# Attention scores of the last four head pairs from float32r parts, in row halves of the array

## The chip, the cores and the metric

The kernel runs on one core of a Trainium2 chip. The metric is the device time of one execution in microseconds. Before the change the median of three runs is 1076.69 us (1075.88 to 1077.53). The profile comes from one execution more, taken by the hardware profiler.

## The reference

For 8 sequences of 448 tokens and 12 heads of 64, a sigmoid attention gives a matrix of 3584 tokens by 768, which goes through two matrix products with a gate between them. All inputs are float32.

```python
# q, k, v: (8, 12, 448, 64)
scores = scale * np.matmul(q, k.transpose(0, 1, 3, 2)) - np.log(S)
attn = 1.0 / (1.0 + np.exp(-scores))
x = np.matmul(attn, v)             # heads side by side: (3584, 768)
h = x @ w_in                       # (768, 2048)
g = h * np.clip(h + 3.0, 0.0, 6.0) / 6.0
out = g @ w_out                    # (2048, 768)
```

## The kernel before

The kernel has three stages, written one after the other, with a hand-written order on each engine (all five are scheduled by the program's own order; each engine works its queue from front to back).

**The attention stage** is the one that the change touches. Heads are taken in pairs: 48 pairs, `p = 0..47`. The tile `qk_p` holds q in one half and k in the other, with the 64 features of the first head on partitions 0 to 63 and those of the second head on 64 to 127. The 448 keys of a head are three blocks of 128 and a rest of 64. A block of a pair is one step; the rests of two pairs (an even and the following odd one) share a step. So two pairs take seven steps (`LC = 7`), and there are 168 steps, `n = 0..167`. `step(n)` gives the pair and the block, or both pairs and `None` for the shared rest. For the last four pairs: 154 to 156 are pair 44, 157 the rests of 44 and 45, 158 to 160 pair 45, 161 to 163 pair 46, 164 the rests of 46 and 47, 165 to 167 pair 47.

`scores(n)` issues four float32 matmuls (L197), each 64 features by 64 keys, one in each quarter of the array (`TILES`: which 64 rows, which 64 columns). They write the tile `sc_n`, of which PSUM holds two. One sigmoid on ACT (L199) turns `sc_n` into `a_n`. `av(n)` issues four float32 matmuls of the same tile size (L214), which multiply `a_n` by the values and accumulate into `pv_p`; it is issued two steps later (`LAG = 2`). The loop over steps says what stands where in every queue:

```python
    for s in range(NS + LAG):
        if s < NS:
            scores(s)
        for f, a in events.pop(s, []):
            f(*a)
        if s >= LAG:
            av(s - LAG)
```

So on PE the order is `sc_n`, `pv` of step n-2, `sc_(n+1)`, `pv` of step n-1. When a pair is complete (with the shared rest for an even one, with its last block for an odd one), `av` also issues a copy `y_p` on ACT (L224) and a sum of `pv_p` and `y_p` into `xr` on DVE (L225). The list `events` holds other work that is hung on a step: the weights' decoding (`decode`), and in the last steps the first three weight splits (`w1_split` of `w_0` to `w_2`), each a cast on ACT (L71) and a subtraction on DVE (L73). `over(on, steps, gen)` advances a generator by one part in each of the steps named.

**The second stage** (first at 261 us) multiplies by `w_in` in a two-by-two scheme with seven products (L359), **the third** (from 667 us) by `w_out` in the same way (L657). Both use float32r: each operand is split by `split` into a part `hi`, rounded to float32r by a cast on ACT, and a part `lo`, the rest, by a subtraction on DVE; three matmuls (hi·hi, hi·lo, lo·hi) of 128 rows by 128 columns then take the place of one float32 matmul.

Tiles that matter here: `temp("qk", 4, ...)`, four buffers of q and k; the tag "T" of `tmp`, three buffers of 128 x 896, used in this stage by `zero` alone and later by `gT`; `ring`, five buffers, used before by the decoded weights and later by the split ones.

Of the kernel before, what the change touches and what calls it, by code (L numbers as in the profile page):

```python
# [8 lines left out]
F32 = mybir.dt.float32  # L9
F32R = mybir.dt.float32r  # L10
# [3 lines left out]
ALU = mybir.AluOpType  # L14
ENG = mybir.EngineType

B, H, S, D = 8, 12, 448, 64
DM, DF = 768, 2048
P = 128
NC = S // P  # L20
NP = H // 2
# [6 lines left out]
LC = 2 * NC + 1  # L28
# [8 lines left out]
halves = (slice(0, D), slice(D, P))  # L37
TILES = ((0, 0), (1, 1), (0, 1), (1, 0))
# [56 lines left out]
def tile_kernel(ctx: ExitStack, tc: tile.TileContext, qk, vP, wi, wo, outT):  # L95
    nc = tc.nc
# [26 lines left out]
    tmp = tmp_ctx.enter_context(tc.tile_pool(name="tmp", bufs=1, side="right"))  # L123
# [17 lines left out]
    def ring(name, shape, dtype):  # L141
        return dw.tile(shape, dtype, tag="ring", name=name, bufs=5)

    def temp(tag, bufs, name, shape=(P, 2, S)):
        return tmp.tile(list(shape), F32, tag=tag, name=name, bufs=bufs)

    def bank(tag, bufs, name):
        return ps.tile([P, 2, 512], F32, tag=tag, name=name, bufs=bufs)
# [18 lines left out]
    def over(when, steps, gen):  # L167
        for n in steps:
            when(n, next, gen, None)

    ops, at, pv, xr = {}, {}, {}, {}

    def load(p):
        b, hp = divmod(p, NP)
        t = temp("qk", 4, f"qk_{p}")
        nc.sync.dma_start(out=t, in_=qk[b, hp])
        if p % 2 == 0:
            v = temp("v", 3, f"v_{p}", (P, 2, LC, D))
            nc.sync.dma_start(out=v, in_=vP[b, hp // 2])
        else:  # L180
            v = ops[p - 1][2]
        ops[p] = t[:, 0], t[:, 1], v

    def step(n):

        m, r = divmod(n, LC)
        return ((2 * m, 2 * m + 1), None) if r == NC else ((2 * m + (r > NC),), r % (NC + 1))

    def scores(n):
        pair, c = step(n)  # L190
        sc = bank("sc", 2, f"sc_{n}")
        for r, j in TILES:
            p = pair[-1 if c is None and r != j else 0]
            q, k, _ = ops[p]
            at_k = slice(NC * P, S) if c is None else slice(c * P + j * D, c * P + (j + 1) * D)
            out = sc[halves[j], int(r != j) if c is None else r, :S]
            nc.tensor.matmul(out, k[halves[r], at_k], q[halves[r]], start=True, stop=True)  # L197
        a = temp("a", 4, f"a_{n}")
        nc.scalar.activation(a, sc[:, :, :S], AF.Sigmoid, bias=bias_s, scale=scale)  # L199
        at[n] = a  # L200

    def av(n):
        pair, c = step(n)
        a = at.pop(n)
        for p in pair:
            if p not in pv:
                pv[p] = bank("pv", 2, f"pv_{p}")
        for r, j in TILES:
            p = pair[-1 if c is None and r != j else 0]
            v = ops[p][2][halves[r], p % 2, 2 * NC if c is None else j * NC + c]  # L210
            whole_first, half_here = p % 2 == 0, (r == j) == (p % 2 == 0)
            first = p % 2 == 1 if c is None else c == 0 and (whole_first or not half_here)
            last = p % 2 == 0 if c is None else c == NC - 1 and not (whole_first and half_here)
            nc.tensor.matmul(  # L214
                pv[p][halves[j], r, :S], v, a[halves[r], int(r != j) if c is None else j], start=first, stop=last
            )
        p = pair[0]
        if c is None or (p % 2 and c == NC - 1):
            b, hp = divmod(p, NP)
            u, k = divmod(hp, KC)  # L220
            if k == 0:
                xr[b, u] = raw(f"xr_{b}_{u}")
            y = temp("y", 2, f"y_{p}", (P, S))
            nc.scalar.copy(y, pv[p][:, 0, :S])  # L224
            nc.vector.tensor_tensor(out=xr[b, u][:, k], in0=pv[p][:, 1, :S], in1=y, op=ALU.add)  # L225
            if k == KC - 1 and b >= 2:
                on(n + LAG + 3, x_store, b, u)
# [92 lines left out]
    for _ in range(WARM):  # L320
        for r, j in TILES:
            nc.tensor.matmul(  # L322
                idle[halves[j], r, :P], zero[halves[r], :D], zero[halves[r]], start=True, stop=True
            )

    load(0)
    load(1)
    for s in range(NS + LAG):
# [6 lines that stand above are left out]
        m, r = divmod(s, LC)  # L335
        if s < NS and r in (0, NC) and 1 < (p := 2 * m + 2 + (r == NC)) < B * NP:
            load(p)
# [219 lines left out]
    for h, n in ((0, 0), (1, 8)):  # L557
        for e in range(2 * EC):
            k, ec = divmod(e, EC)
# [9 lines left out]
    for k, i in enumerate(PHASES[1:]):  # L569
        n = 8 * (k + 1)  # L570
# [56 lines left out]
    for n, (i, p, h) in enumerate(units):  # L627
# [24 lines left out]
        x = gx.pop(n)  # L652
        for ec in range(EC):
            w = w2[i, h, ec]
            for c in range(FC):
                for wk, xk in ((0, 0), (0, 1), (1, 0)):
# [4 lines left out]
                        start=h == 0 and c == 0 and xk == 0 and wk == 0,  # L661
                        stop=h == 1 and c == FC - 1 and wk == 1,
# [37 lines left out]
```

## Time and profile before

The profiled execution took 1077.52 us, of which the span from its first to its last instruction is 1075.7 us; the median of the runs is 1076.69 us. Times in the views are microseconds from the start of the span.

| stage, us from the start | length | PE busy | DVE busy | ACT busy | POOL busy |
|---|---|---|---|---|---|
| attention, 0 to 261.1 | 261.1 | 258.70 | 163.85 | 215.84 | 39.42 |
| first product, 261.1 to 666.7 | 405.6 | 403.73 | 313.89 | 220.07 | 128.76 |
| second product, 666.7 to 1075.7 | 409.0 | 404.55 | 265.28 | 125.33 | 6.02 |

Names in the views: PE is TensorE's matmuls, PEld its weight loads, DVE VectorE, ACT ScalarE, POOL GpSimd, SP the engine that issues DMAs. A row of the timeline has the start, the length, the engine, the line of the program, the operation, what it writes and reads, shapes, and how many instructions were merged into the row; in brackets stands idle time of the engine before it and what ended it. The ends of matmuls are modelled, their starts are recorded. A row of a group has busy time and mean length (ns) behind the bar.

### The profile page before, as it was taken

What the parts mean: (1) busy time and instruction counts of PE and PEld (TensorE: products, weight loads), DVE (VectorE), ACT (ScalarE), POOL (GpSimd) and SP (SyncE); (2) the same over time, 40 slices, a digit from 0 to 9 for tenths busy, and PEclk for the clock granted to TensorE, in tenths of its full rate; (3) what the DMA queues carried; (4) which work ended last, traced back from release to release, by engine and by line L of the source; (5) the groups of instructions that cost most, each with busy time, mean ns of one, the idle gap of its engine ahead of it and who ended that gap; (6) DMA issues with size and microseconds to landing.
All of it is one profiled execution on the core that took longest, in us unless ns stands there. A gap on an engine that the chain in (4) does not pass through costs nothing.

```text
span 1075.7 us, 16712 instructions
## 1 busy us (share of the span) xinstructions
PE 1067.0 (99%) x6784; PEld 890.4 (83%) x6784; DVE 743.0 (69%) x713; ACT 561.2 (52%) x612; POOL 174.2 (16%) x82
## 2 busy tenths in 40 slices
PE   9999999999999999999999999999999999999998
PEld 4443466666999989999999999998999999999998
DVE  4679856642577987799888665987864437787642
ACT  7888988886446554664465555434332313222420
POOL 0214130000143345235322221200000000000000
PEclk9999999999999999999999999999999999999999
DMA  8887998874666877688766878869885376898741
GB/s 323 299 306 275 336 350 320 312 269 154 248 213 207 295 250 229 204 283 272 233 190 213 286 238 280 303 268 319 328 314 190 111 273 222 287 347 287 272 147 52
DMA packets 81484, 277.13 MB, mean 258 GB/s; under 512 B 7936, under 2 KB 22272, under 8 KB 81408
## 3 DMA queue, kind: packets, MB, share of 16 engines
q1 hardware_dynamic: 81408, 276.07, 73.0%
q8 instruction: 53, 0.87, 0.3%
q14 instruction: 23, 0.19, 0.0%
HBM read 189.92 MB, written 86.11 MB: 257 GB/s over the span
## 4 chain that ended last, share of the span: by engine, by line
PE 88%; DVE 4%; DMA 4%; issue 2%; ACT 2%; SPq 0%; ACTq 0%; DVEq 0%
PE po L657 32%; PE A L359 19%; PE sc L197 11%; PE pv L214 11%; PE D L359 9%; PE B L359 5%; DMA ws<-dw 2%; PE pl L657 1%; DVE w L73 1%; DMA dw<-w2S 1%; DMA qk<-qk 0%; ACT gx L71 0%; DVE x L73 0%; ACT a L199 0%; PE idle L322 0%
## 5 line engine op out<-in xcount | busy, mean ns | idle before, releaser
L657 PE MATMUL po<-gx,w 128*128 128x448 f32 x1944 | 390.0, 362 | 1.0 <-ACT w L71 0.7
L657 PEld LDWEIGHTS po<-gx,w 128*128 128x128 f32 x1944 | 364.3, 188 | 26.6 <-DVE w L73 1.4
L359 PE MATMUL A<-x,w 128*128 128x448 f32 x1152 | 236.1, 362 | 1.9 <-ACT u L384 1.9
L359 PEld LDWEIGHTS A<-x,w 128*128 128x128 f32 x1152 | 215.9, 188 | 17.6 <-ACT u L384 2.6
L71 ACT CAST gx<-gr 128x1792 fp32r<-128x1792 f32 x56 | 94.8, 1695 | 204.8 <-PE po L657 113.1
L214 PE MATMUL pv<-a,v 64*64 64x448 f32 x1344 | 198.8, 537 | 1.0 <-DVE xr L225 0.6
L197 PE MATMUL sc<-qk 64*64 64x448 f32 x1344 | 198.3, 537 | 0.4 <-ACT a L199 0.4
L199 ACT ACTIVATE a<-sc,bias_s 128x896 f32<-128x896 f32 x168 | 168.3, 1009 | 44.2 <-PE sc L197 41.3
L73 DVE TENSOR_TENSOR w<-ws,w 128x768 fp32r<-128x768 f32 x112 | 148.9, 1338 | 26.3 <-ACT w L71 26.0
L73 DVE TENSOR_TENSOR gx<-gr,gx 128x1792 fp32r<-128x1792 f32 x56 | 113.3, 2023 | 77.3 <-ACT gx L71 77.2
L214 PEld LDWEIGHTS pv<-a,v 64*64 64x64 f32 x1344 | 70.1, 133 | 62.8 <-issue 38.9
L197 PEld LDWEIGHTS sc<-qk 64*64 64x64 f32 x1344 | 69.3, 133 | 61.9 <-issue 29.2
L359 PE MATMUL D<-x,w 128*128 128x448 f32 x576 | 120.4, 362 | 0.0
L359 PEld LDWEIGHTS D<-x,w 128*128 128x128 f32 x576 | 108.1, 188 | 7.1
L71 ACT CAST w<-ws 128x768 fp32r<-128x768 f32 x112 | 93.0, 830 | 32.2 <-DMA ws<-dw 32.1
L393 POOL TENSOR_TENSOR gT<-g,g 128x896 f32<-128x896 f32 x16 | 43.5, 2721 | 269.7 <-DVE g L370 269.7
L225 DVE TENSOR_TENSOR xr<-pv,y 128x448 f32<-128x448 f32 x48 | 29.8, 621 | 53.7 <-ACT y L224 53.7
L359 PE MATMUL B<-x,w 128*128 128x448 f32 x288 | 60.2, 362 | 0.0
L379 ACT ACTIVATE g<-cD,bias 128x896 f32<-128x896 f32 x32 | 33.5, 1045 | 46.6 <-DVE cD L388 24.8
L359 PEld LDWEIGHTS B<-x,w 128*128 128x128 f32 x288 | 54.0, 188 | 3.6
L384 ACT COPY u<-A 128x896 f32<-128x896 f32 x32 | 29.0, 907 | 45.6 <-PE A L359 45.6
L388 DVE TENSOR_TENSOR cD<-D,u 128x896 f32<-128x896 f32 x32 | 34.8, 1088 | 21.0 <-ACT u L384 13.0
(65 smaller groups left out, 773.7 us busy)
## 6 DMA issues: line engine op xcount, KB each, us to landing
gr<-gd SPq DMA_DIRECT2D x56, 896.0 KB, 5.6
ws<-dw SPq DMA_DIRECT2D x112, 384.0 KB, 3.9
gd<-g SPq DMA_DIRECT2D x64, 448.0 KB, 4.6
qk<-qk SPq DMA_DIRECT2D x48, 448.0 KB, 6.7
gd<-gT SPq DMA_DIRECT2D x32, 448.0 KB, 5.2
gr<-gd SPq DMA_DIRECT2D x32, 448.0 KB, 6.1
wi<-wi SPq DMA_DIRECT2D x16, 768.0 KB, 8.0
wo<-wo SPq DMA_DIRECT2D x24, 512.0 KB, 5.2
```

The lines of the kernel that those rows point to most:

```text
L71: nc.scalar.copy(hi, a)
L73: nc.vector.tensor_tensor(out=lo, in0=a, in1=hi.bitcast(F32), op=ALU.subtract)
L197: nc.tensor.matmul(out, k[halves[r], at_k], q[halves[r]], start=True, stop=True)
L199: nc.scalar.activation(a, sc[:, :, :S], AF.Sigmoid, bias=bias_s, scale=scale)
L214: nc.tensor.matmul(pv[p][halves[j], r, :S], v, a[halves[r], int(r != j) if c is None else j], start=first, stop=last)
L225: nc.vector.tensor_tensor(out=xr[b, u][:, k], in0=pv[p][:, 1, :S], in1=y, op=ALU.add)
L359: nc.tensor.matmul(t[:, j, :S], w[:, wk, j, kc], x[:, xk, kc], start=i in (M1, M2, M5) and m == 0, stop=m == 3 * KC - 1, skip_group_check= ...
L379: nc.scalar.activation(r, h, AF.Relu, bias=bias_3, scale=1.0)
L384: nc.scalar.copy(acc[key, q], acc["A", q][:, :, :S])
L388: nc.vector.tensor_tensor(out=c, in0=acc[name, q][:, :, :S], in1=acc[key, q], op=ALU.add)
L393: nc.gpsimd.tensor_tensor(out=t3, in0=quad[q, B22], in1=quad[q, B12], op=ALU.subtract)
L657: nc.tensor.matmul(po[p][ec] if n > len(units) - 3 else po[p][:, ec, :S], w[:, wk, c], x[:, xk, c], start=h == 0 and c == 0 and xk == 0 an ...
```

## The change

For the last four pairs (44 to 47) the scores of the whole blocks are computed in the way of the later stages. `part(p)` makes, for q and k of a pair, a rounded part `hi` (two casts on ACT, tag "T") and the rest `lo` (two subtractions on DVE, in `ring`). It is hung on the two steps ahead of the pair's first block: casts at step n-2, subtractions at step n-1. `scores(n)` then issues six float32r matmuls of 64 rows by 128 columns: hi·hi, hi·lo (of q), lo (of k)·hi, for each of the two heads, whose rows are the two halves of the array; each head writes its own bank of `sc_n`, where before each head wrote both halves of the partitions in 64 columns each. Twelve steps are so changed: 154 to 156, 158 to 163 and 165 to 167. The two shared steps (157 and 164), the sigmoid, `av` and everything behind stay; DMAs are issued in the same order.

```diff
+    def part(p):
+        t = ops[p]
+        hi = tmp.tile([P, 2, S], F32R, tag="T", name=f"hi_{p}", bufs=3)
+        lo = ring(f"lo_{p}", [P, 2, S], F32R)
+        for k in range(2):
+            nc.scalar.copy(hi[:, k], t[k])
+        yield
+        for k in range(2):
+            nc.vector.tensor_tensor(out=lo[:, k], in0=t[k], in1=hi[:, k].bitcast(F32), op=ALU.subtract)
+        parts[p] = hi, lo
+        yield
...
     def scores(n):
         pair, c = step(n)
         sc = bank("sc", 2, f"sc_{n}")
-        for r, j in TILES:
-            p = pair[-1 if c is None and r != j else 0]
-            q, k, _ = ops[p]
-            at_k = slice(NC * P, S) if c is None else slice(c * P + j * D, c * P + (j + 1) * D)
-            out = sc[halves[j], int(r != j) if c is None else r, :S]
-            nc.tensor.matmul(out, k[halves[r], at_k], q[halves[r]], start=True, stop=True)
+        if c is not None and pair[0] in parts:
+            x = parts[pair[0]]
+            for m, (wk, xk) in enumerate(((0, 0), (0, 1), (1, 0))):
+                for r in range(2):
+                    nc.tensor.matmul(
+                        sc[:, r, :S],
+                        x[wk][halves[r], 1, c * P : (c + 1) * P],
+                        x[xk][halves[r], 0],
+                        start=m == 0,
+                        stop=m == 2,
+                    )
+        else:
...
+    for p in range(B * NP - 4, B * NP):
+        n = LC * (p // 2) + (NC + 1) * (p % 2)
+        over(on, (n - 2, n - 1), part(p))
     load(0)
```

How the queues change. Names carry the pair or step and then a running number of the program; the brackets say on whose semaphores a row waits, and line numbers differ between the two programs.

PE at steps 153 to 155, before:

```order
L197 MATMUL sc_153_2573<-qk_43_2439 64x448 x3
L214 MATMUL pv_43_2564<-a_151_2550,v_42_2390 64x448 x4
L197 MATMUL sc_154_2585<-qk_44_2496 64x448 [waits DMAHW2_49,Activation_49]
L197 MATMUL sc_154_2585<-qk_44_2496 64x448 x3
L214 MATMUL pv_43_2564<-a_152_2562,v_42_2390 64x448 x4
L197 MATMUL sc_155_2600<-qk_44_2496 64x448 [waits Activation_49]
```

and PE at the same place in the changed program:

```order
L238 MATMUL pv_43_2568<-a_151_2550,v_42_2390 64x448 x4
L208 MATMUL sc_154_2591<-hi_44_2564 128x448 [waits PE_49,Activation_49]
L208 MATMUL sc_154_2591<-hi_44_2564 128x448
L208 MATMUL sc_154_2591<-lo_44_2565,hi_44_2564 128x448 [waits DVE_49]
L208 MATMUL sc_154_2591<-lo_44_2565,hi_44_2564 128x448
L208 MATMUL sc_154_2591<-hi_44_2564,lo_44_2565 128x448 [waits DVE_49]
L208 MATMUL sc_154_2591<-hi_44_2564,lo_44_2565 128x448
L238 MATMUL pv_43_2568<-a_152_2562,v_42_2390 64x448 x4
L208 MATMUL sc_155_2608<-hi_44_2564 128x448 [waits Activation_49]
```

The group of `sc_154` is of another tile size than the two `pv` groups beside it, and waits on ACT for `hi` and twice on DVE, for `lo` of q and for `lo` of k; `pv` of step 152 stands behind it. The wait on PE itself is for `sc_152`, the tile's earlier writer.

ACT around step 152, before (a is the sigmoid's result, y the copy of a finished pair):

```order
L199 ACTIVATE a_151_2550<-sc_151_2545,bias_s_170 128x896 [waits PE_49,Activation_49]
L199 ACTIVATE a_152_2562<-sc_152_2557,bias_s_170 128x896 [waits PE_49,Activation_49]
L224 COPY y_42_2570<-pv_42_2525 128x448 [waits DVE_49,PE_49]
L199 ACTIVATE a_153_2578<-sc_153_2573,bias_s_170 128x896 [waits PE_49,Activation_49]
L199 ACTIVATE a_154_2590<-sc_154_2585,bias_s_170 128x896 [waits PE_49,Activation_49]
```

and in the changed program:

```order
L223 ACTIVATE a_152_2562<-sc_152_2557,bias_s_170 128x896 [waits PE_49,Activation_49]
L189 CAST hi_44_2564<-qk_44_2496 128x448 [waits DMAHW2_49]
L189 CAST hi_44_2564<-qk_44_2496 128x448
L248 COPY y_42_2574<-pv_42_2525 128x448 [waits DVE_49,PE_49]
L223 ACTIVATE a_153_2582<-sc_153_2577,bias_s_170 128x896 [waits PE_49,Activation_49]
```

The two casts of pair 44 now stand between the sigmoid of step 152 and the copy of pair 42.

DVE from pair 42's sum on, in the changed program (before, the four sums of `xr` followed each other with nothing between them):

```order
L249 TENSOR_TENSOR xr_7_0_2573<-pv_42_2525,y_42_2574 128x448 [waits Activation_49]
L192 TENSOR_TENSOR lo_44_2565<-qk_44_2496,hi_44_2564 128x448 [waits DMAHW2_49]
L192 TENSOR_TENSOR lo_44_2565<-qk_44_2496,hi_44_2564 128x448
L249 TENSOR_TENSOR xr_7_0_2573<-pv_43_2568,y_43_2621 128x448 [waits Activation_49]
L192 TENSOR_TENSOR lo_45_2634<-qk_45_2543,hi_45_2633 128x448 [waits DMAHW4_49,DMAHW1_49,Activation_49]
L192 TENSOR_TENSOR lo_45_2634<-qk_45_2543,hi_45_2633 128x448 [waits Activation_49]
L249 TENSOR_TENSOR xr_7_0_2573<-pv_44_2637,y_44_2692 128x448 [waits Activation_49]
L192 TENSOR_TENSOR lo_46_2684<-qk_46_2604,hi_46_2683 128x448 [waits DMAHW7_49]
L192 TENSOR_TENSOR lo_46_2684<-qk_46_2604,hi_46_2683 128x448
```

The subtractions of pair 44 stand behind the sum of pair 42, and those of pair 46 behind the sum of pair 44; those of pair 45 follow a sum whose copy came before the casts of pair 45.

More of the change, by code (lines that the diff above doesn't have):

```diff
@@ L169, in over @@
             when(n, next, gen, None)
-    ops, at, pv, xr = {}, {}, {}, {}
+    ops, at, pv, xr, parts = {}, {}, {}, {}, {}
     def load(p):
@@ L191, in scores @@
         sc = bank("sc", 2, f"sc_{n}")
-        for r, j in TILES:
-            p = pair[-1 if c is None and r != j else 0]
-            q, k, _ = ops[p]
-            at_k = slice(NC * P, S) if c is None else slice(c * P + j * D, c * P + (j + 1) * D)
-            out = sc[halves[j], int(r != j) if c is None else r, :S]
-            nc.tensor.matmul(out, k[halves[r], at_k], q[halves[r]], start=True, stop=True)
+        if c is not None and pair[0] in parts:
[10 more added lines that the diff above has]
+        else:
+            for r, j in TILES:
+                p = pair[-1 if c is None and r != j else 0]
+                q, k, _ = ops[p]
+                at_k = slice(NC * P, S) if c is None else slice(c * P + j * D, c * P + (j + 1) * D)
+                out = sc[halves[j], int(r != j) if c is None else r, :S]
+                nc.tensor.matmul(out, k[halves[r], at_k], q[halves[r]], start=True, stop=True)
         a = temp("a", 4, f"a_{n}")
```

## The prediction

> **What bounds the kernel now.** First I read the page from the top: span, busy shares, the forty slices, and the chain that ended last.
>
> ```profile
> span 1075.7 us, 16712 instructions
> ...
> PE 1067.0 (99%) x6784; PEld 890.4 (83%) x6784; DVE 743.0 (69%) x713; ACT 561.2 (52%) x612; POOL 174.2 (16%) x82
> ...
> PE   9999999999999999999999999999999999999998
> ...
> PEclk9999999999999999999999999999999999999999
> ...
> PE 88%; DVE 4%; DMA 4%; issue 2%; ACT 2%; SPq 0%; ACTq 0%; DVEq 0%
> ```
>
> TensorE is busy everywhere, at the full granted clock, and is 88% of the chain. What is added to it, or makes it wait, reaches the end of the kernel unless it was waiting there already. So the next view is the stretch that holds the changed steps, by engine.
>
> ```profile
> core 0: us, PE busy (x) PEld busy (x) DVE busy (x) ACT busy (x) POOL busy (x), PEclk, DMA share, GB/s
> 225.00:255.40 30.40, 30.40 (x328) 19.22 (x324) 9.33 (x16) 23.16 (x27) 0.00 (x0) 1.00 0.51 187
> ```
>
> PE has no gap there, while DVE and ACT have room. Then the timelines of ACT and of PE around step 154, the first changed one.
>
> ```profile
> 235.90 1.01 ACT L199 ACTIVATE a<-sc,bias_s 128x896 f32<-128x896 f32 x1 [0.50 <-PE sc L197]
> 236.81 0.52 ACT L224 COPY y<-pv 128x448 f32<-128x448 f32 x1
> 237.41 1.01 ACT L199 ACTIVATE a<-sc,bias_s 128x896 f32<-128x896 f32 x1
> 238.91 1.01 ACT L199 ACTIVATE a<-sc,bias_s 128x896 f32<-128x896 f32 x1 [0.50 <-PE sc L197]
> ```
>
> ```profile
> 237.41 0.54 PE L197 MATMUL sc<-qk 64*64 64x448 f32 x2
> 237.51 0.54 PE L214 MATMUL pv<-a,v 64*64 64x448 f32 x2
> 237.79 0.64 PE L197 MATMUL sc<-qk 64*64 64x448 f32 x4
> 238.16 0.54 PE L214 MATMUL pv<-a,v 64*64 64x448 f32 x2
> 238.26 0.54 PE L197 MATMUL sc<-qk 64*64 64x448 f32 x2
> ```
>
> Counted back from the last sigmoid (a_167, at 259.12 below), the three sigmoids are a_152, a_153, a_154: a step takes 1.50 us, and a sigmoid waits for its scores. A float32 matmul is two instructions, so the eight sc instructions here are step 154. Each holds a quarter of the array for 0.375 us (237.41 to 237.79), so a group of eight costs 0.75, and a step, one sc group and one pv group, twice that. The pv rows start between the sc rows: the two groups share the array with no gap. The last pair of sc_154 streams until 238.26 + 0.375 = 238.64, and a_154 starts 0.27 later.
>
> The end of the stage is different:
>
> ```profile
> 255.45 1.01 ACT L199 ACTIVATE a<-sc,bias_s 128x896 f32<-128x896 f32 x1 [0.50 <-PE sc L197]
> 256.35 0.82 ACT L71 CAST w<-ws 128x768 fp32r<-128x768 f32 x1
> 257.07 1.01 ACT L199 ACTIVATE a<-sc,bias_s 128x896 f32<-128x896 f32 x1
> 257.97 0.83 ACT L71 CAST w<-ws 128x768 fp32r<-128x768 f32 x1
> 258.69 0.54 ACT L224 COPY y<-pv 128x448 f32<-128x448 f32 x1
> 259.12 1.03 ACT L199 ACTIVATE a<-sc,bias_s 128x896 f32<-128x896 f32 x1
> ```
>
> From a_165 on ACT runs without a gap, 1.62 us to a_166 and 2.05 more to a_167, and PE waits for a_167. So what happens to PE after sc_165 is largely covered. Ten changed sc groups (154 to 156, 158 to 163 and 165) lie on the path, and two (166, 167) under ACT.
>
> **The change, part by part.** *Streams.* The nearest float32r matmuls are those of the next stage:
>
> ```profile
> 264.99 3.60 PE B L359 x18
> ```
>
> That is 0.20 us each for 448 columns. Six matmuls, two at a time in the two row halves, are 3 × 0.20 = 0.60 in place of 0.75. No row shows 64 rows by 128 columns in float32r; the ends are 3 × 0.19 = 0.56 (half of the 0.375 above, one pass) and 6 × 0.20 = 1.20 (the halves in turn). I take 0.60, since quarters with different rows do run together above.
>
> *Change of tile size.* Each new sc group now stands between pv groups of 64 × 64 tiles. The trace has one place where the tile size changes, at the end of the stage:
>
> ```profile
> 260.19 0.21 PEld L214 LDWEIGHTS pv<-a,v 64*64 64x64 f32 x8 [1.12 <-ACT a L199]
> 260.62 0.56 PE L214 MATMUL pv<-a,v 64*64 64x448 f32 x4
> 261.11 0.19 PEld L359 LDWEIGHTS A<-x,w 128*128 128x128 f32 x1 [0.71 <-issue]
> 261.11 0.47 PE L359 MATMUL A<-x,w 128*128 128x448 f32 x1
> ```
>
> The last pv matmul begins at 260.62 + 0.56 - 0.54 = 260.64 and streams until 261.02. The first weight load of the other size comes only at 261.11, after 0.71 us in which the loader waited for nothing shown; the first matmul, 0.47 long where 0.36 is usual, really starts 0.11 after it. So the switch costs 0.09 + 0.11 = 0.20. A lone pv group, from its first weight load (260.19) to its last stream (261.02), takes 0.82. A new step is then 0.82 + 0.09 for pv and 0.11 + 0.60 + 0.09 for sc, 1.71 in place of 1.50: **0.21 lost in each of ten steps**, although the streams are shorter. The low end is no cost at all (weights loaded ahead, as among the quarters): 0.75 + 0.60 = 1.35, 0.15 won. I take the row that shows a switch.
>
> The page TensorEngine Tiling of the Trainium skill (Key Properties) says that a change of tiling mode, and not of tile alone, drains TensorE. By it 64 × 128 beside 64 × 64 is such a change too, which no row here shows; the one switch in the trace agrees, at 0.20 us. It speaks against the change, and against the first rival below.
>
> *Making the parts.* Eight casts on ACT and eight subtractions on DVE, 128x448 each. Nearest rows:
>
> ```profile
> L71 ACT CAST gx<-gr 128x1792 fp32r<-128x1792 f32 x56 | 94.8, 1695 | 204.8 <-PE po L657 113.1
> ...
> L73 DVE TENSOR_TENSOR w<-ws,w 128x768 fp32r<-128x768 f32 x112 | 148.9, 1338 | 26.3 <-ACT w L71 26.0
> ...
> L71 ACT CAST w<-ws 128x768 fp32r<-128x768 f32 x112 | 93.0, 830 | 32.2 <-DMA ws<-dw 32.1
> ...
> L225 DVE TENSOR_TENSOR xr<-pv,y 128x448 f32<-128x448 f32 x48 | 29.8, 621 | 53.7 <-ACT y L224 53.7
> ```
>
> (1695 - 830)/1024 is 0.845 ns an element, so a cast of 448 takes 830 - 320 × 0.845 = 0.56 us; back to back, ACT starts the next 0.10 before the last ends (256.35 to 257.07 above for a cast of 0.82). A subtraction I put at 0.62, as L225 of the same size, the next starting 0.05 early. The upper end is the L73 row, the same operation, scaled: 1338 × 448/768 = 0.78, which would add 0.3 at each pair, 1.2 in all; the lower is 0.57 each, 0.4 less in all. As busy time all this hides in the idle shares above. Its **order** does not hide.
>
> Pair 44: behind a_152 (235.90) ACT does hi q from 236.81, hi k from 237.27 to 237.83, and only then the copy y_42, from 237.73 to 238.25, which before began at 236.81. DVE has the sum of y_42 ahead of the subtractions: it runs from 238.29 to 238.91, lo q from 238.86 to 239.48, lo k from 239.43 to 240.05. PE reaches sc_154 at about 238.0 (the pv row of 237.51 streams until 237.88, and the switch) and does the first product; the second waits for lo q, the third needs lo k as weights: load at 240.10, stream from 240.21 to 240.41. Before, sc_154 was through at 238.64: 1.75 late. Queued behind it on PE are pv of step 152, sc_155 and all the rest, and nothing of the 1.75 comes back, since PE had no gap.
>
> Pair 46 (sc_161) has the same order, counted from a_159 at time T: hi k ends at T + 1.93, y_44 at 2.35, its sum at 3.0, lo k at 4.15, sc_161 at 4.5. sc_159 ended at T - 0.27, so sc_161 ends 4.8 after it, where before it was 3.0: 1.75 again (two steps of 1.71 alone would be 0.41).
>
> Pairs 45 and 47: no copy or sum stands between the casts and the subtractions. From a_156, lo q starts at T + 1.5, lo k ends at 2.7, sc_158 at 3.05, which is 3.3 after sc_156 where two steps were 3.0: 0.3, of which the switches are 0.2.
>
> Sum, as lateness against before: sc_154 1.75; sc_155 and 156 0.42; sc_158 0.3; sc_159 0.21; sc_161 1.75; sc_162 and 163 0.42; sc_165 0.3; together 5.15. Under ACT at the end, a_166 now waits for a step of 1.71 where ACT took 1.62: 0.09. **Total +5.2 us.** Behind it PE works as before, with the same queues, and 5.2 us later. The profiled execution took 1077.52 us, 0.83 above the median of 1076.69; 1082.7 on it is 1081.9 as a median.
>
> **Rivals.** *One: switching is free.* Steps of 1.35: the waits for lo stay, as PE only comes earlier to them. sc_154 +1.75, then -0.3, +0.3, -0.15, +1.75, -0.3, +0.3: +3.3, or 1080.0. For it: weights are loaded ahead among the quarters. Against it: the gap of 0.71 on the weight loader. Chance 0.13.
>
> *Two: weights of the next product are not loaded during the one before*, so a round of two matmuls takes 0.31: sc 0.93, step 0.91 + 0.93 + 0.09 = 1.93, 0.43 more than before. This hides where PE waits for lo anyway (sc_154, sc_161), and counts in the others: 1.75, 0.86, 0.42, 0.43, 1.75, 0.86, 0.42 in the order of the sum, and 0.31 at the end, +6.8, or 1083.5. Against it: the B matmuls come every 0.20 with loads of 0.188 between them. The page TensorE: Matmul & The Clock Gate (Part 3, The mechanism) says that weight loads overlap matmuls only where the row group differs, which would give this, though it also knows of a background buffer for weights; the B rows here, where all 128 rows are used by each, don't agree with the first. Chance 0.10.
>
> *Three: the row halves run in turn.* Step 0.91 + 0.11 + 1.20 + 0.09 = 2.31, 0.8 more in each: sc_154 1.9, sc_155 and 156 1.6, sc_158 0.8, sc_159 0.8, sc_161 1.9, sc_162 and 163 1.6, sc_165 0.8, 1.0 at the end: +10.4, 1087. Chance 0.06.
>
> *Four, not slower: the parts are there in time and switching is free.* Ten steps win 0.15 each, the last two are under ACT: -1.5, 1075.2, within 0.2%, and at 0.56 a group 1074.8. It decides itself at lo k of pair 44: done before 238.4, it costs nothing; I find 240.05, and no duration above can be 1.6 us wrong. Chance 0.03. With switches at their price and the parts in time: +2.2, 1078.9; chance 0.04. That the change doesn't take effect is excluded: the order shows the new matmuls in all twelve steps.
>
> **How the numbers follow.** My forecast has 0.64, at 1081.9. The range 1079.0 to 1085.0 takes in rivals one and two and the bounds of subtractions and switches, and leaves out three, four, and part of the tails. A measurement of this kernel can tell about 0.2% (2.15 us) from no change. Slower by more than that means above 1078.85: my case, one, two, three and half of the last, 0.91 less something for what lies behind the stage, 0.88. Within 0.2%: 0.10. Faster: twelve groups at 0.56 would win 2.2 at the very most: 0.02.
>
> **What would show it.** In the profile of the changed kernel: two waits of PE for DVE of over 1 us, at sc_154 and sc_161, and hardly any at sc_158 and sc_165; weight-load gaps at each new group, and a_155 to a_156 1.7 us apart rather than 1.35 or 2.3; the chain entering L192 and L189 there; a first A matmul about 5 us later, and from it the same spacing to the end. I am wrong if subtractions come before y's sum, if steps are 1.35 apart, or if the stage behind takes up some of the delay.

## The result

The changed kernel takes 1082.01 us (median of 4 runs, 1081.23 to 1083.93) against 1076.38 (4 runs, 1075.88 to 1077.53): the ratio is 1.0052, with a 95% interval of 1.0037 to 1.0068. It is slower by about 5.6 us (4.0 to 7.3 by the interval); 5.2 were forecast. A second set of runs, told below as an experiment, gave 1.0045 (1.0033 to 1.0058). The ratios leave out one slow execution of the kernel before, among the runs that the last three experiments are compared with: it took 1551.40 us at a granted clock of 0.655.

The page after, for the lines shown of before (the profiled execution took 1081.23 us):

```profile
span 1079.1 us, 16686 instructions
...
PE 1070.4 (99%) x6760; PEld 868.6 (80%) x6760; DVE 753.0 (70%) x721; ACT 565.2 (52%) x620; POOL 173.2 (16%) x82
...
PE   9999999999999999999999999999999999999998
...
PEclk9999999999999999999999999999999999999999
...
PE 91%; DVE 4%; DMA 2%; issue 1%; ACT 1%; SPq 0%; ACTq 0%; DVEq 0%
```

At this grain hardly anything shows: TensorE is as busy as before, and the clock is full. The stretch of the changed steps does show it (the window is shifted by 0.13 us, by which a_152 starts later here, at 236.04 in place of 235.90):

```profile
core 0: us, PE busy (x) PEld busy (x) DVE busy (x) ACT busy (x) POOL busy (x), PEclk, DMA share, GB/s
225.13:255.53 30.40, 28.54 (x262) 11.92 (x258) 12.02 (x21) 22.23 (x29) 0.00 (x0) 1.00 0.50 182
```

PE was busy for all of 30.40 us there and is now for 28.54, while it gets through fewer steps. The chain of work that ended last stays on PE in this stretch of the kernel before (224.90 to 255.36). Now, in order of time (start, length, what), it leaves PE ahead of sc_154:

```profile
236.94 0.55 ACT hi L189
237.49 0.37 issue
237.86 0.54 ACT y L248
238.40 0.02 issue
238.43 0.62 DVE xr L249
239.05 1.08 DVE lo L192 x2
240.13 0.04 issue
240.18 0.47 PE sc L208 x2
240.64 0.91 PE pv L238 x8
```

Cast, copy of the finished pair, its sum, the two subtractions, and then the third product of sc_154: the order that the queues were read to have. The timeline of PE has the first groups of the pairs 44 (sc_154), 45 (sc_158) and 46 (sc_161), and between them the end of sc_159, a group without a wait:

```profile
239.64 0.47 PE L208 MATMUL sc<-lo,hi 64*128 64x448 f32 x2 [1.05 <-DVE lo L192]
240.18 0.47 PE L208 MATMUL sc<-hi,lo 64*128 64x448 f32 x2
...
246.92 0.42 PE L208 MATMUL sc<-hi,lo 64*128 64x448 f32 x2
...
248.69 0.36 PE L208 MATMUL sc<-hi,lo 64*128 64x448 f32 x2
...
252.76 0.47 PE L208 MATMUL sc<-lo,hi 64*128 64x448 f32 x2 [0.68 <-DVE lo L192]
253.30 0.47 PE L208 MATMUL sc<-hi,lo 64*128 64x448 f32 x2
```

sc_154 and sc_161 wait long for DVE, and sc_158 only by the 0.06 that its third product (246.92) is longer than the usual 0.36. And the weight loads around the plain steps 159 and 160:

```profile
248.18 0.19 PEld L208 LDWEIGHTS sc<-hi 64*128 64x128 f32 x2 [0.70 <-issue]
248.29 0.19 PEld L208 LDWEIGHTS sc<-lo,hi 64*128 64x128 f32 x2
248.49 0.19 PEld L208 LDWEIGHTS sc<-hi,lo 64*128 64x128 f32 x2
248.98 0.21 PEld L238 LDWEIGHTS pv<-a,v 64*64 64x64 f32 x8 [0.30 <-issue]
249.89 0.19 PEld L208 LDWEIGHTS sc<-hi 64*128 64x128 f32 x2 [0.70 <-issue]
```

From group to group (248.18 to 249.89) a step is 1.71 us: 0.80 for the new scores and 0.91 for the values. Two matmuls are merged in each row of PE, one in each row half, and a pair of them follows every 0.20 us, so the row halves do run together. The second and third loads come while the product before them runs (0.20 apart). At each change of size the loader stands still with nothing to wait for that the profile shows, 0.70 and 0.30 us. Most of that is time in which the weights loaded last are still in use: the third product of sc_159 streams from 248.69 to 248.89, and the first load of the other size follows 0.09 later, at 248.98. What a change of size costs is this 0.09 and the load behind it, by which the row of the first product is longer (0.47 for 0.36 at a new group, so 0.11).

### The profile page after: what moved, and what is told of

It reads as the page before. It is cut to its first block, busy times and chain, and to the rows that moved or that the text cites. A ratio compares the mean times of both kernels' runs of the same rounds, so it can differ in the third digit from the quotient of the medians.

```text
span 1079.1 us, 16686 instructions
## 1 busy us (share of the span) xinstructions
PE 1070.4 (99%) x6760; PEld 868.6 (80%) x6760; DVE 753.0 (70%) x721; ACT 565.2 (52%) x620; POOL 173.2 (16%) x82
## 4 chain that ended last, share of the span: by engine, by line
PE 91%; DVE 4%; DMA 2%; issue 1%; ACT 1%; SPq 0%; ACTq 0%; DVEq 0%
PE po L684 32%; PE A L386 20%; PE pv L238 11%; PE D L386 10%; PE sc L221 10%; PE B L386 5%; PE pl L684 1%; DMA ws<-dw 1%; DMA dw<-w2S 1%; PE sc L208 1%; DVE w L73 1%; ACT gx L71 0%; PE idle L346 0%; DVE x L73 0%; DVE wA L57 0%
## 5 line engine op out<-in xcount | busy, mean ns | idle before, releaser
L238 PE MATMUL pv<-a,v 64*64 64x448 f32 x1344 | 186.4, 538 | 0.6 <-DVE xr L249 0.6
L221 PE MATMUL sc<-qk 64*64 64x448 f32 x1248 | 174.6, 537 | 0.4 <-ACT a L223 0.4
L73 DVE TENSOR_TENSOR w<-ws,w 128x768 fp32r<-128x768 f32 x112 | 154.4, 1386 | 20.5 <-ACT w L71 20.2
L238 PEld LDWEIGHTS pv<-a,v 64*64 64x64 f32 x1344 | 60.9, 133 | 73.3 <-issue 69.0
L221 PEld LDWEIGHTS sc<-qk 64*64 64x64 f32 x1248 | 58.0, 133 | 66.0 <-issue 42.6
```

The source lines that it names most:

```text
L73: nc.vector.tensor_tensor(out=lo, in0=a, in1=hi.bitcast(F32), op=ALU.subtract)
L238: nc.tensor.matmul(pv[p][halves[j], r, :S], v, a[halves[r], int(r != j) if c is None else j], start=first, stop=last)
```

## The experiments

To compare stages without the chances of the rest of the run, each experiment's profile was also read for one stretch: from the start of a_152 to the first weight load of the second stage. In the changed kernel these are:

```profile
236.04 1.01 ACT L223 ACTIVATE a<-sc,bias_s 128x896 f32<-128x896 f32 x1 [0.49 <-PE sc L221]
...
266.31 0.30 PEld L386 LDWEIGHTS A<-x,w 128*128 128x128 f32 x2 [0.70 <-issue]
```

The stretch is 261.11 - 235.90 = 25.21 us in the kernel before and 266.31 - 236.04 = 30.27 in the changed one: **5.06 us late**. The theory under test (A) is the prediction's: about 3 us are waits for late parts, about 2.1 us are the switches of tile size.

**Parts made two steps earlier** (e1_early).

```diff
-        over(on, (n - 2, n - 1), part(p))
+        over(on, (n - 4, n - 3), part(p))
```

> The parts of each pair are made two steps earlier (casts at step n-4, subtractions at n-3), nothing else differs from the changed kernel. Theory A (3.0 us of the loss are waits of PE for the late lo parts, 2.1 us are switches of the tile size): the waits of PE for DVE in the first group of a pair vanish, steps still take 1.71 us, the first product of the second stage starts about 2.2 us later than in the kernel before, in place of 5.2; median about 1078.6. Theory B (the loss is in the new groups themselves, about 0.45 us in each of twelve): the first product stays about 5 us late, median about 1082.

Measured: 1078.41 us (11 runs) against 1076.22 for the kernel before, ratio 1.0017 (1.0008 to 1.0025). PE at sc_158 in this kernel:

```profile
244.59 0.47 PE L208 MATMUL sc<-hi 64*128 64x448 f32 x2
244.91 0.36 PE L208 MATMUL sc<-lo,hi 64*128 64x448 f32 x2
245.11 0.37 PE L208 MATMUL sc<-hi,lo 64*128 64x448 f32 x2
245.41 0.98 PE L238 MATMUL pv<-a,v 64*64 64x448 f32 x8
246.32 0.47 PE L208 MATMUL sc<-hi 64*128 64x448 f32 x2
```

No row of PE waits for DVE any more, and the step is still 1.73 here (244.59 to 246.32). The stretch is 263.12 - 235.87 = 27.25, 2.04 late. So 3.0 of the 5.06 were the late parts, and theory B, by which nothing would have changed, falls.

**Subtractions ahead of the sum** (e2_order): the casts stay late, only the order on DVE changes.

```diff
-        over(on, (n - 2, n - 1), part(p))
+        over(on, (n - 2, n - 2), part(p))
```

> Subtractions hung on the same step as the casts (n-2), so that they stand ahead of the sum of the finished pair on DVE; the casts stay where they were. Theory A with the order of DVE as its cause: the two long waits, at sc_154 and sc_161, fall to what sc_158 and sc_165 show (0.1 us), the first product starts about 2.5 us late, median about 1079. Rival C (the casts are what is late, wherever the subtractions stand): the long waits stay above 1 us, and the first product stays about 5 us late.

Measured: 1078.28 us (10 runs), ratio 1.0020 (1.0011 to 1.0029). DVE at step 152 in this kernel:

```profile
237.87 1.16 DVE L192 TENSOR_TENSOR lo<-qk,hi 128x448 fp32r<-128x448 f32 x2 [2.90 <-ACT hi L189]
238.95 0.62 DVE L249 TENSOR_TENSOR xr<-pv,y 128x448 f32<-128x448 f32 x1
```

The subtractions start with the first cast's end, and the sum stands behind them. On PE, sc_154 is now:

```profile
238.77 0.37 PE L208 MATMUL sc<-lo,hi 64*128 64x448 f32 x2
239.09 0.47 PE L208 MATMUL sc<-hi,lo 64*128 64x448 f32 x2
```

The third product starts 0.32 after the second, where 0.20 is usual: 0.1 us of wait. At sc_161 the two are 0.20 apart, with no wait left. The stretch is 263.96 - 236.38 = 27.58, 2.37 late. The casts were not too late by themselves; the copy and the sum between them and the subtractions were. Rival C falls.

**Parts made and not used** (e3_unused). The scores leave out the parts: they are float32 in quarters, as in the kernel before.

```diff
-        if c is not None and pair[0] in parts:
+        if False:
```

> The parts are made where the changed kernel makes them, but no matmul uses them: all scores are float32 in quarters as before, so casts, subtractions and their buffers are extra work. Theory A: this work is hidden, PE never waits for it; the first product of the second stage starts within 0.3 us of the kernel before, median 1076.4. Rival D (ACT and DVE become the bound when the parts are added): the first product starts 1 us or more late.

Measured: 1077.15 us (10 runs), ratio 1.0006 (0.9995 to 1.0018), which takes in no change, with a wide spread (1074.67 to 1080.04). The stretch is 261.36 - 236.15 = 25.21: not late at all. Busy time from 225 to 255 us in this kernel:

```profile
225.20:255.60 30.40, 30.40 (x326) 19.52 (x322) 13.84 (x24) 26.25 (x35) 0.00 (x0) 1.00 0.54 194
```

DVE (13.84) and ACT (26.25) carry the extra work, PE has no gap. It is hidden, and rival D falls; the spread of the times lies elsewhere, behind this stage or in other runs than the profiled one, and isn't explained.

**Only the tile size** (e4_halves_f32): float32, no parts, two row halves in place of four quarters.

```diff
-        if c is not None and pair[0] in parts:
-            x = parts[pair[0]]
...
+        if c is not None and pair[0] >= B * NP - 4:
+            q, k, _ = ops[pair[0]]
+            for r in range(2):
+                nc.tensor.matmul(
+                    sc[:, r, :S], k[halves[r], c * P : (c + 1) * P], q[halves[r]], start=True, stop=True
+                )
...
-    for p in range(B * NP - 4, B * NP):
-        n = LC * (p // 2) + (NC + 1) * (p % 2)
-        over(on, (n - 2, n - 1), part(p))
```

> No parts at all: the scores of the same twelve steps as float32 matmuls of 64 rows by 128 keys in the two row halves, two matmuls a step (four instructions) in place of four (eight); so only the tile size differs from the kernel before. Theory A (the switch of the tile size costs, whatever the type): a score group streams 0.75 us, a step takes 0.91 + 0.11 + 0.75 + 0.09 = 1.86 us, 0.36 over the 1.50 before; ten steps on the path and 0.24 at the end, the first product starts about 3.8 us late, median about 1080.2. Rival E (what costs is the change of type between float32 and float32r): steps stay at 1.50, the first product starts at the same time, median 1076.4.

Measured: 1079.20 us (8 runs), ratio 1.0027 (1.0017 to 1.0038). Weight loads in this kernel:

```profile
247.87 0.21 PEld L233 LDWEIGHTS pv<-a,v 64*64 64x64 f32 x8 [0.65 <-issue]
...
248.78 0.30 PEld L207 LDWEIGHTS sc<-qk 64*128 64x128 f32 x4 [0.70 <-issue]
...
249.73 0.21 PEld L233 LDWEIGHTS pv<-a,v 64*64 64x64 f32 x8 [0.65 <-issue]
```

The loader stands still at each change of size here too, with one type throughout, and a step of 1.86 us (247.87 to 249.73). The stretch is 264.84 - 235.87 = 28.97, 3.76 late, where 3.8 was expected. So the tile size costs this without a change of type, and rival E falls. The size brings with it half as many matmuls, each writing all 128 partitions of its bank; these were not taken apart from it. The median rose by 3.0 us (1.8 to 4.1 by the interval), where 1080.2, or 4.0 more, was expected.

**Half the switches** (e5_runs2): on top of the early parts, score groups in runs of two, then two value groups.

```diff
-    for s in range(NS + LAG):
-        if s < NS:
-            scores(s)
...
+    while s < NS + LAG:
+        run = (s, s + 1) if s in (154, 158, 160, 162, 165) else (s,)
+        for i in run:
+            if i < NS:
+                scores(i)
...
+        for i in run:
+            if i >= LAG:
+                av(i - LAG)
```

> Parts early as in the first experiment, and the score groups of two steps issued one behind the other, then the two value groups (steps 154 and 155, 158 and 159, 160 and 161, 162 and 163, 165 and 166), with the same matmuls. Theory A (the price is one per switch of the tile size, 0.2 us): two steps cost 0.11 + 1.20 + 0.09 and 0.82 + 0.75 + 0.09, 3.06 us in place of 3.42, against 3.00 in float32; the first product starts about 0.5 us later than before, where the parts made early alone gave 2.0; median about 1076.7. Rival F (the price belongs to each new group, for its type or its weight loads): the first product stays about 2 us late, median 1078.4.

Measured: 1076.83 us (11 runs) against 1076.32, ratio 1.0004 (0.9995 to 1.0013). Weight loads of one run of two:

```profile
244.61 0.18 PEld L208 LDWEIGHTS sc<-hi 64*128 64x128 f32 x2 [0.70 <-issue]
...
245.12 0.19 PEld L208 LDWEIGHTS sc<-hi 64*128 64x128 f32 x2
...
246.04 0.21 PEld L238 LDWEIGHTS pv<-a,v 64*64 64x64 f32 x8 [0.31 <-issue]
...
247.70 0.18 PEld L208 LDWEIGHTS sc<-hi 64*128 64x128 f32 x2 [0.70 <-issue]
```

The second group's first load (245.12) comes without a standstill, as size and place in the array stay; two steps take 3.09 (244.61 to 247.70). The stretch is 262.01 - 236.23 = 25.78, 0.57 late. The same twelve new groups cost 2.04 us when each stands alone, and 0.57 when they stand in seven groups of one or two. So the price hangs on the switch, and rival F falls. This is the best of the versions with the new scores; it does not beat the kernel before.

**Both kernels once more** (e6_after_again, e7_before_again), without an edit.

> The changed kernel once more, for a second profile and more times. Theory A: the first product starts 5.0 to 5.2 us later than in the kernel before, in any run, and the median lies 5.2 above it. What its profile gave back in the second stage (1.8 us of the 5.2, at a product that waited for a load of weights in the kernel before and not here) is then chance of that one profile, and differs here. Rival G (the later start of the second stage makes that wait shorter each time): the median lies only 3.4 to 3.7 above.

> The kernel before once more, for a second profile: whether PE waits there for the load of weights at 376 us (2.0 us) and at 479 us (0.6 us) each time. Theory A: these waits come and go, as the times of the kernel before are spread over 4 us. Rival G: they are there again, of the same length.

Measured: the changed kernel 1081.33 us (5 runs), ratio 1.0045 (1.0033 to 1.0058), its stretch 265.96 - 235.67 = 30.29, 5.08 late; the kernel before 1075.80 (11 runs), its stretch 261.02 - 235.81 = 25.21. Between the first two profiles the spans differ by only 3.4 (1075.7 and 1079.1), though the stretch is 5.06 longer. The rows of the page for the product A, with idle time behind the second bar: first profile of before, first of after, second of before:

```profile
L359 PE MATMUL A<-x,w 128*128 128x448 f32 x1152 | 236.1, 362 | 1.9 <-ACT u L384 1.9
```

```profile
L386 PE MATMUL A<-x,w 128*128 128x448 f32 x1152 | 236.0, 362 | 0.1
```

```profile
L359 PE MATMUL A<-x,w 128*128 128x448 f32 x1152 | 236.0, 362 | 0.2 <-ACT u L384 0.2
```

The 1.9 us of idle time in the first profile of before are two waits, of 1.64 us at 376.6 and 0.23 at 479.3. The chain of that profile shows the first of them behind a load of weights:

```profile
365.02 11.45 DMA ws<-dw
376.54 0.83 ACT w L71
377.37 0.81 ACT u L384
378.23 11.08 PE A L359 x54
```

None of the other eight profiles of this study has more than 0.2 us of such idle time. The second profile of before has a span of 1073.9, and the two of after have 1079.1 and 1078.7, which is 5.2 and 4.8 more. So nothing to speak of was given back behind the changed steps; the first profile had a wait that its own program does not show again, and rival G falls by the profiles. The times alone (4.8 us more, 3.6 to 6.2 by the interval) would hardly have told it from its 3.4 to 3.7. Why the load of weights was late that once is not shown.

## Why the prediction was right

**The bound.** PE has no slack at the changed steps, so each delay went through to the first product, and from there, the 1.9 us of waits in one profile aside, to the end.

**Streams.** Taken as 0.60 a group, the halves together: the rows of after are 0.20 apart, with two matmuls each. The third rival (the halves in turn) would have shown 2.31 us a step.

**Tile size.** The one switch in the trace of before was read as 0.20 us, a step as 1.71; it is 1.71, and e4 shows the same price in float32. The first rival (switching is free) would have shown 1.35. The second rival (no loads ahead) falls to the loads 0.20 apart, each in a row half that is streaming. The page TensorEngine Tiling of the Trainium skill (Key Properties) says that a change of tiling mode drains TensorE; this case's trace agrees for 64 × 128 beside 64 × 64, where the first load of the other size comes 0.09 us after the last stream, in both directions. The page TensorE: Matmul & The Clock Gate of the Trainium skill (Part 3, The mechanism) says that weight loads overlap matmuls only where the row group differs, though it also knows of a background buffer for weights. This case's trace does not agree with the first, since the loads at 248.29 and 248.49 use the rows of the product that streams at the time.

**Order.** sc_154 was put 1.75 late, and sc_161 1.75 in place of 0.41 for its two steps. The sigmoids give 1.70 (a_154 at 240.74, less 0.13, against 238.91) and 1.71 (from a_159 at 249.16 to a_161 at 253.87 are 4.71, where 3.00 was usual). The sign named for it, waits of over 1 us, reads 1.05 and 0.68 in the two rows; the third product then waits 0.34 more in each (its start is 0.54 after the second's, where 0.20 is usual), so that both come to over 1 us. Casts of 0.55 and two subtractions in 1.16 are as scaled. A side effect that the prediction didn't name, that the sigmoid behind casts and copy starts 0.75 late (a_153 at 238.29), cost PE nothing: it is there in e3_unused too, which wasn't late. The branch of the fourth rival with the parts in time and the switches at their price was put at 2.2; e1_early is that kernel, and its stretch is 2.04 late.

**The end.** The tail was put at 0.09 for two whole steps. In the changed kernel:

```profile
260.57 1.01 ACT L223 ACTIVATE a<-sc,bias_s 128x896 f32<-128x896 f32 x1 [0.45 <-PE sc L208]
...
262.28 1.01 ACT L223 ACTIVATE a<-sc,bias_s 128x896 f32<-128x896 f32 x1
...
264.33 1.02 ACT L223 ACTIVATE a<-sc,bias_s 128x896 f32<-128x896 f32 x1
```

a_165 to a_166 takes 1.71 where it took 1.62, and from there to a_167 2.05 as before: 0.09, and the rest is covered by ACT.

**Where it was off.** The forecast summed to 5.2 at the first product, against 5.06; the two long waits came out at 1.70 and 1.71 in place of 1.75, and the rest nearly as summed. The weak step is the last one, from this delay to the time of a run. The sum was added to a profiled execution that took 1077.52 us and gave 1082.7 for it; the profiled execution of the changed kernel took 1081.23. The one that was summed against had 1.9 us of waits behind loads of weights, which its second profile doesn't have. Taking off 0.83 to reach the median put that partly right. That the median of 1082.01 agrees with the forecast of 1081.9 to 0.1 us is partly luck, since the medians themselves move by more than that between sets: 1076.69, 1076.38 and 1076.22 for the kernel before, 1082.01 and 1081.33 for the changed one. One sum of the chances is wrong as well: the cases counted as slower, with half of the last, come to 0.64 + 0.13 + 0.10 + 0.06 + 0.02 = 0.95, and not to 0.91.

## What to carry to other kernels

A change that shortens TensorE's streams can lose if it alternates with neighbours of another tile size: here each new group saved 0.15 us of stream, and paid 0.36 around it: twice the 0.09 between a stream and the next load, and the two first loads, 0.11 for the new group and 0.07 for the other. By these numbers, as an estimate, it wins from three such groups in a run on (0.45 saved for 0.36 paid); a run of two lost 0.09 (3.09 against 3.00), and three were not run.

Work that is hidden by its amount can still stall the bound engine by its place. Read each queue for what stands between the parts of a handover, here a copy and a sum that belonged to another pair.

Compare two profiles over the changed stretch, between two instructions that both kernels have, before the whole spans are compared.

## What the runs showed of the hardware

The price of a change of tile size is the same with float32 on both sides (a step of 1.86 us in place of 1.50 in e4_halves_f32) as between float32 and float32r (1.71 us in place of the 1.35 of its streams): 0.36 us for a change there and back. The weight loader's idle time for the same two changes is longer (0.70 and 0.30 us, and 0.70 and 0.65 in e4_halves_f32), since it includes time in which the weights loaded last are still being used. Two float32r matmuls in the row halves, with all 128 columns, run together and take the 0.20 us that one full-array matmul takes in the next stage (18 in 3.60 us). No run here has float32r in the four quarters, where the tile size would not change.
